# A decode kernel whose cache loads span two heads of one batch, regrouped to one head of both batches

## The chip, the cores and the metric

The kernel runs on one core of one Trainium2 chip. The metric is the time of one execution on the device in microseconds (us); lower is better. The core has five engines: TensorE (PE in the profile), VectorE (DVE), ScalarE (ACT), GpSimd (POOL) and SyncE (SP), and 16 DMA engines that move data between the chip's memory (DRAM tensors) and the on-chip buffers. SP and ACT each issue transfers into a queue of their own.

## The reference

One decoding step of an attention layer followed by a feed-forward layer, for a batch of two, one new token each. All data is float32.

```python
B, Sq, D = 2, 1, 512
H, Sk, Dh = 32, 8192, 128
# k_cache, v_cache: (B, H, Sk, Dh); wq: (D, H*Dh); wo: (H*Dh, D)
q = (layernorm(x) @ wq).reshape(B, Sq, H, Dh).transpose(0, 2, 1, 3)
scores = einsum("bhqd,bhkd->bhqk", q, k_cache) * Dh ** -0.5
o = einsum("bhqk,bhkd->bhqd", softmax(scores), v_cache)
h = x + o.transpose(0, 2, 1, 3).reshape(B, Sq, H * Dh) @ wo
h2 = h + (silu(layernorm(h) @ w_gate) * (layernorm(h) @ w_up)) @ w_down
```

One head of one batch has 8192 x 128 x 4 B = 4 MiB of keys and as much of values. There are 64 such pairs of head and batch, so keys and values together are 512 MiB, and each byte of them is used once. In the cache the batch is the slowest dimension: the heads of one batch lie one behind the other, 4 MiB apart, and the same head of the two batches is 128 MiB apart.

## The kernel before

**Units.** The work on the cache is cut into U = 32 units. A unit is two (head, batch) pairs: 128 partitions, of which the lower 64 hold one pair and the upper 64 the other. Within a pair, the 8192 positions are dealt to 64 partitions, 128 consecutive positions each; so one partition gets one unbroken run of 128 x 128 x 4 B = 64 KiB. Before the change, unit i is the heads 2m and 2m + 1 of batch b, with m = i // 2 and b = i % 2. Since two neighbouring heads of a batch lie one behind the other in the cache, the unit's 128 runs are one unbroken block of 8 MiB.

**Buffers.** Keys have two slots of 8 MiB (`kslot0`, `kslot1`, used in turn), values one (`vslot`). The last unit's values go into a key slot.

**What one unit does.** VectorE multiplies the key tile by the query (L435, two halves), sums over the head's dimension (L439), tells SP that the slot is free (L441, semaphore `kfree`), and takes the maximum (L442, L420). TensorE moves the maxima across partitions (L371 to L374), ScalarE computes the exponentials (L468), TensorE multiplies them with the value tile (`pe_values`, L381), ScalarE tells SP that the value slot is free (L480, semaphore `vfree`), and the result is scaled and written as a column of `oT` (L485). The loops over units are hardware loops; an iteration of VectorE's and ScalarE's holds two units, one for each key slot.

**Before and after the units.** A layer norm and the query projection (L352) fill `qsb`, which holds each query row repeated over the 64 partitions of its pair. After the last unit come the output projection with `wo`, a second layer norm, and the feed-forward layer with `w_gate`, `w_up` and `w_down`; their weights are loaded into the slots as these come free.

**What sets the order.** All large loads stand in one list, and SP issues them one after the other into its one queue (L650): `wq`, the first keys in two halves, then keys of unit i and values of unit i - 1 in turn, the last values, `wo`, `w_gate`, `w_up`, `w_down`. Ahead of a load that overwrites a slot, SP waits for the slot's semaphore (`kfree` or `vfree`); everything behind it in the list waits too. The access pattern of the source is made by `k_src` (L154), for keys and values alike. Of the other transfers, the input `xs` is loaded by ACT (L252) as 2 rows of 2 KiB, and the output is stored by SP and ACT (L657) as 2 rows of 1 KiB each.

Of the kernel before, what the change touches and what calls it, by code (L numbers as in the profile page):

```python
# [4 lines left out]
AF = mybir.ActivationFunctionType  # L5
# [6 lines left out]
P = 128  # L12
# [3 lines left out]
class Program:  # L16
# [22 lines left out]
    def do(self, engine, fn, sem=None, by=1):  # L39

        if sem is None:
            self.steps[engine].append(fn)
            return None
        self.count[sem] += by
        self.steps[engine].append(lambda e: fn(e).then_inc(sem, by))
        return sem, self.count[sem]
# [8 lines left out]
def decode_block(nc, x, k_cache, v_cache, wq, wo, w_gate, w_up, w_down, out):  # L55
    B, _, D = x.shape
    _, H, S, DH = k_cache.shape
    F = w_gate.shape[1]
    assert DH == P and B == 2 and D == 512 and F == 14 * P and H == 32 and S == 64 * P
    DC = D // P  # L60
# [3 lines left out]

    HP = P // 2
    NJ = S // HP
    U = B * H // 2
    LANE = 1
    COLS = (0, 2, 1, 3)
    MQ = H // 2  # L70
    HALF = (slice(0, HP), slice(HP, P))


# [7 lines left out]
    def sbuf(name, *shape, align=32):  # L81
        return nc.alloc_sbuf_tensor(name, list(shape), F32, align_bytes=align).ap()
# [7 lines left out]
    vslot = sbuf("vslot", P, SLOT, align=512)  # L90
# [12 lines left out]
    oT = sbuf("oT", P, H, B)  # L103
    hT = sbuf("hT", P, DC, 32)
    xT = sbuf("xT", P, DC, B)
    osb = sbuf("osb", P, W * DH)
    qsb = sbuf("qsb", P, B, MQ, DH)
    oq = sbuf("oq", P, H, B)
    scores = [sbuf(f"s{n}", P, NJ) for n in range(2)]
    m1 = sbuf("m", P, 1)  # L110
# [24 lines left out]
    wait, do = g.wait, g.do  # L135


    s_dve, s_act, s_pe, s_pool = (g.sem(n) for n in ("dve", "act", "pe", "pool"))
# [13 lines left out]
    loads = []  # L152

    def k_src(cache, i):  # L154
        m, b = divmod(i, B)
        return cache[b, 2 * m : 2 * m + 2].rearrange("h (p j) d -> (h p) (j d)", p=HP)

    v_last = kslot[U % 2]

    def load_kv(kind, i, parts=1):  # L160
        cache, t = (k_cache, kslot[i % 2]) if kind == "k" else (v_cache, vslot if i < U - 1 else v_last)
        n = SLOT // parts
        for c in range(parts):
            own = parts > 1 or (kind, i) == ("v", U - 1)
            sem = alone(f"{kind}{i}_{c}") if own else s_k[i % 2] if kind == "k" else s_v
            loads.append(((kind, i), c, t[:, c * n : (c + 1) * n], k_src(cache, i)[:, c * n : (c + 1) * n], sem))

    loads.append((("wq", 0), 0, vslot, wq.rearrange("(p c) m -> p (c m)", p=P), s_v))
    load_kv("k", 0, 2)
# [132 lines left out]
    _, p = layernorm(xs, [(x_in, 16)])  # L302
# [28 lines left out]
    p = do("vector", lambda e: e.tensor_copy(xT, yt), s_dve)  # L331
# [5 lines left out]
        s_dve,  # L337
    )
    wait("tensor", xb_done, landed[("wq", 0), 0])
    wqv = vslot.rearrange("p (c m k d) -> p c k m d", c=DC, k=2, d=DH)  # L340
    q_done = []
    for n, (m, b) in enumerate((m, b) for m in range(0, MQ, 4) for b in range(B)):
        ps = wide[n % 2].rearrange("p (j d) -> p j d", d=DH)
        if n == 7:
            stop(1)
        if n > 1:
            wait("tensor", q_done[n - 2])
        for c in range(DC):
            for k in range(2):
                p = do(  # L350
                    "tensor",
                    lambda e, ps=ps, c=c, k=k, m=m, b=b: e.matmul(  # L352
                        ps[HALF[k]],
                        xb[:, c * B + b, :],
                        wqv[:, c, k, m : m + 4, :],
                        start=(c == 0),
                        stop=(c == DC - 1),
                    ),
                    s_pe if c == DC - 1 and k == 1 else None,
                )  # L360
        wait("scalar", p)
        q_done.append(
            do("scalar", lambda e, ps=ps, m=m, b=b: e.activation(qsb[:, b, m : m + 4, :], ps, AF.Copy), s_act)
        )
    freed["wq", 0] = p
    wait("tensor", consts_done)

# [58 lines left out]
    def dve_unit(e, b, q, first, done, seen):  # L426
        n = NJ // 2
        s = scores[b]
        for c in range(2):
            if first:  # L430
                e.wait_ge(*landed[("k", 0), c])
            elif c == 0:
                e.wait_ge(s_k[b], 16)
            kt = kslot[b][:, c * n * DH : (c + 1) * n * DH].rearrange("p (j d) -> p j d", d=DH)
            e.tensor_tensor(kt, kt, q.to_broadcast([P, n, DH]), op=OP.mult).then_inc(s_own_dve, 1)  # L435
            if not first:
                (recip if c else biggest)(e, seen + c + 1)
            e.wait_ge(s_own_dve, done + 2 * c + 1)
            e.tensor_reduce(s[:, c * n : (c + 1) * n], kt, axis=AX.X, op=OP.add).then_inc(s_own_dve, 1)  # L439
        e.wait_ge(s_own_dve, done + 4)  # L440
        e.sem_inc(s_kfree, 1)  # L441
        e.tensor_reduce(m1, s, axis=AX.X, op=OP.max).then_inc(s_dve_pe, 1)  # L442

    def dve_rounds(e):
        dve_unit(e, 0, qsb[:, 0, 0:1, :], True, 0, 0)
        e.wait_ge(*q_done[-1])
        e.sem_inc(s_own_dve, -4)
        with nc.Fori(0, U // 2 - 1, engines=[DVE]) as m:  # L448
            dve_unit(e, 1, qsb[:, 1, bass.ds(m, 1), :], False, 0, 0)
            dve_unit(e, 0, qsb[:, 0, bass.ds(m + 1, 1), :], False, 4, 2)  # L450
            e.sem_inc(s_own_dve, -8)
            e.sem_inc(s_pe_dve, -4)
            for k in range(2):
                e.sem_inc(s_k[k], -16)
        dve_unit(e, 1, qsb[:, 1, U // 2 - 1 : U // 2, :], False, 0, 0)
        biggest(e, 3)
        recip(e, 4)

# [19 lines left out]
    def outputs(e, o, told, seen):  # L478
        e.wait_ge(s_pe_act, seen)
        e.sem_inc(s_vfree, 1)  # L480
        e.activation(osb, opart, AF.Copy)  # L481
        e.wait_ge(s_dve_act, told)
        e.activation(rdiag, diag, AF.Copy, scale=r).then_inc(s_act_pe, 1)  # L483
        e.wait_ge(s_pe_act, seen + 1)
        return e.activation(o, ot_ps, AF.Copy)  # L485

    def act_rounds(e):
        with nc.Fori(0, U // 2 - 1, engines=[ACT]) as m:
            for b in range(B):
                softmax(e, b, b + 1, 3 * b + 1)  # L490
                outputs(e, oT[:, bass.ds(m * 2, 2), b], b + 1, 3 * b + 2)
            e.sem_inc(s_own_act, -2)
            e.sem_inc(s_dve_act, -2)
            e.sem_inc(s_pe_act, -6)
        for b in range(B):
            softmax(e, b, b + 1, 3 * b + 1)
            if b:
                e.activation(warm, mhalf[:1, :], AF.Sigmoid)
            last = outputs(e, oT[:, H - 2 :, b], b + 1, 3 * b + 2)
        last.then_inc(s_oT, 1)  # L500

    wait("scalar", consts_done)
# [1 line left out]
    for i in range(U):  # L504
# [5 lines left out]
    p = do(  # L510
        "vector",
        lambda e: e.tensor_tensor(
            om,
            oT.rearrange("p h b -> p b h")[:, :, :, None].to_broadcast([P, B, H, NQ]),
            quarter[:, None, None, :].to_broadcast([P, B, H, NQ]),
            op=OP.mult,
        ),
        s_dve,
    )
    wait("tensor", p)  # L520
    for b in range(B):
        p = do(
            "tensor",
            lambda e, b=b: e.matmul(
                oq_ps[:, b, :], om[:, b].rearrange("p h q -> p (h q)"), fold, start=True, stop=True
            ),
            s_pe if b == B - 1 else None,
        )
    wait("scalar", p)
    p = do("scalar", lambda e: e.activation(oq.rearrange("p c b -> p b c"), oq_ps, AF.Copy), s_act)  # L530
    wait("tensor", p, zeroed)
    for c in range(H):
        for e_, (c0, n) in enumerate(WO):
            if c0 == c:
                wait("tensor", landed[("wo", 0), e_])
        t = c % 4
        p = do(
            "tensor",
            lambda e, c=c, t=t: e.matmul(
                wide[0][32 * t : 32 * t + B, :],  # L540
                oq[:, c, :],
                wo_t[:, c * D : (c + 1) * D],
                start=(c < 4),
                stop=(c >= H - 4),
            ),
# [4 lines left out]
    p = do("scalar", lambda e: e.activation(osb, wide[0], AF.Copy), s_act)  # L550
# [34 lines left out]
    p = project_f(0, gate)  # L585
# [3 lines left out]
    for t in range(4):  # L589
        do(  # L590
            "tensor",
            lambda e, t=t: e.matmul(
                f_ps[32 * t : 32 * t + 32, :], place, h1[:, COLS[t] * P : (COLS[t] + 1) * P], start=True, stop=False
            ),
# [3 lines left out]
    p = do("scalar", lambda e: e.activation(sg, gate, AF.Sigmoid), s_act)  # L598
    wait("vector", p)
    sg_done = do("vector", lambda e: e.tensor_mul(sg, gate, sg), s_dve)  # L600
    p = project_f(DC, up)
# [4 lines left out]
    p = do(  # L606
        "vector",
        lambda e: e.tensor_mul(
            gu.rearrange("p (c j) -> p j c", c=FB),
            up.rearrange("p (j c) -> p j c", c=FB),  # L610
            sg.rearrange("p (j c) -> p j c", c=FB),
        ),
        s_dve,
    )
    gT = rest[:, D + 2 * FQ : D + 3 * FQ]
    wait("vector", p)
    p = do("vector", lambda e: e.transpose(gT, gu), s_dve)
# [3 lines left out]
    for c in range(FB):  # L621
# [3 lines left out]
        for t in range(4):  # L625
            p = do(
                "tensor",
                lambda e, c=c, t=t: e.matmul(  # L628
                    f_ps[32 * t : 32 * t + 32, :],
                    gT[:, c * 32 : (c + 1) * 32],  # L630
                    wd_t[:, c * D + COLS[t] * P : c * D + (COLS[t] + 1) * P],
                    start=False,
                    stop=(c == FB - 1),
                ),
# [73 lines left out]
```

## Time and profile before

| what | value |
|---|---|
| time, median of 3 runs | 1309.12 us (1309.05 to 1309.28) |
| the profiled execution's own time | 1309.09 us |
| its span, first to last instruction | 1307.7 us |
| DMA queue of SP, share of the 16 engines' span | 99.7% |
| bytes moved, mean rate | 564.77 MB, 432 GB/s |
| VectorE busy | 1131.1 us (86%) |
| TensorE busy | 434.1 us (33%) |
| ScalarE busy | 81.0 us (6%) |

The span leaves out 1.39 us of the execution's own time (1309.09 - 1307.7). A row of a group of instructions gives its line, engine, operation, output and inputs, the shape and the count, then the busy time in us and the mean of one in ns, then the idle time of the engine ahead of it and what ended it. "q1" is SP's queue of transfers, "q10" ACT's; packets are what the 16 DMA engines executed, with the small ones counted by size. In the table of stretches the last two columns are the share of the 16 DMA engines that was busy (an average over engines and over the stretch) and the rate in GB/s. In the list of transfers the last column is the median time from issue to landing.

### The profile page before, as it was taken

The numbers are of one execution on the slowest core, as the hardware profiler recorded it, in microseconds if no ns is written. First come the engines' busy times: TensorE is split into PE (matmuls) and PEld (weight loads), VectorE is DVE, ScalarE is ACT, GpSimd is POOL, SyncE is SP. The second block draws the span as 40 slices with busy tenths as digits, with TensorE's granted clock in tenths as the row PEclk, the third lists the DMA queues.
The fourth block names the chain that finished last, engine by engine and source line by source line (L and its number), as shares of the span: only waits on it lengthen the run. The fifth ranks groups of instructions, "written<-read, shape, count | busy, mean of one in ns | idle before, by whom it ended". The sixth has DMA issues, their size and how long they took to land.

```text
span 1307.7 us, 7046 instructions
## 1 busy us (share of the span) xinstructions
PE 434.1 (33%) x2956; PEld 136.0 (10%) x2956; DVE 1131.1 (86%) x246; ACT 81.0 (6%) x272; POOL 3.1 (0%) x15
## 2 busy tenths in 40 slices
PE   2633223333213333322333321333331233332177
PEld 1210001011001011000101100101100010110022
DVE  0999988899888889888889988888988888998841
ACT  0100000000000000000000000000000000000010
POOL 0000000000000000000000000000000000000000
PEclk9866566666556666556666655666665666665578
DMA  9999999999999999999999999999999999999998
GB/s 402 437 439 431 439 433 435 439 429 439 427 439 427 441 425 441 431 439 431 437 437 431 439 427 439 427 441 425 441 429 441 431 437 437 429 441 427 439 419 377
DMA packets 10963, 564.77 MB, mean 432 GB/s; under 512 B 1222, under 2 KB 1226, under 8 KB 1612
## 3 DMA queue, kind: packets, MB, share of 16 engines
q1 hardware_dynamic: 10948, 564.67, 99.7%
q8 instruction: 5, 0.08, 0.0%
q14 instruction: 2, 0.02, 0.0%
q10 hardware_dynamic: 8, 0.01, 0.0%
HBM read 564.66 MB, written 0.00 MB: 432 GB/s over the span
## 4 chain that ended last, share of the span: by engine, by line
DMA 53%; DVE 45%; PE 1%; issue 0%; DVEq 0%; SPq 0%; ACTq 0%
DMA kslot<-in_A_k_cache_dram 48%; DVE kslot L435 22%; DVE s L439 22%; DMA kslot<-in_A_v_cache_dram 3%; DMA kslot<-in_B_w_down_dram 3%; PE opart L381 1%; DVE gm L420 0%; SPq L650 0%; DVE r L424 0%; PE bank L628 0%; DVEq L435 0%; DVEq L441 0%; DVE kslot L642 0%; DVE m L442 0%; DVEq L448 0%
## 5 line engine op out<-in xcount | busy, mean ns | idle before, releaser
L435 DVE TENSOR_TENSOR kslot<-kslot,qsb 128x8192 f32<-128x8192 f32 x64 | 555.6, 8681 | 108.8 <-DMA kslot<-in_A_k_cache_dram 95.5
L439 DVE TENSOR_REDUCE s<-kslot 128x64 f32<-128x8192 f32 x64 | 555.2, 8675 | 0.1
L381 PE MATMUL opart<-vslot,pz 128*8 128x512 f32 x1984 | 284.6, 738 | 239.9 <-DMA vslot<-in_A_v_cache_dram 239.9
L373 PE MATMUL bank<-gm,nscale 1*64 1x1 f32 x64 | 11.8, 251 | 353.6 <-DVE gm L420 353.6
L381 PEld LDWEIGHTS opart<-vslot,pz 128*8 128x8 f32 x1984 | 55.1, 103 | 443.2 <-DMA vslot<-in_A_v_cache_dram 242.5
L371 PE MATMUL bank<-ident,m 128*1 128x128 f32 x64 | 18.7, 396 | 165.6 <-DVE m L442 165.6
L481 ACT ACTIVATE osb<-opart 128x512 f32<-128x512 f32 x32 | 19.1, 598 | 557.3 <-PE opart L381 557.3
L373 PEld LDWEIGHTS bank<-gm,nscale 1*64 1x64 f32 x64 | 9.1, 200 | 369.6 <-DVE gm L420 369.6
L393 PE MATMUL bank<-rdiag,osb 128*128 128x2 f32 x256 | 34.0, 255 | 40.0 <-ACT rdiag L483 40.0
L465 ACT ACTIVATE nb<-bank 128x1 f32<-128x1 f32 x32 | 5.5, 172 | 541.3 <-PE bank L374 541.3
L393 PEld LDWEIGHTS bank<-rdiag,osb 128*128 128x128 f32 x256 | 31.2, 192 | 69.6 <-ACT rdiag L483 69.6
L376 PE MATMUL bank<-rs,sides 128*128 128x1 f32 x64 | 18.7, 362 | 41.6 <-ACT pz L468 41.6
L352 PE MATMUL wide<-vslot,osb 128*64 128x512 f32 x128 | 29.7, 626 | 3.5 <-DMA vslot<-in_A_wq_dram 3.5
L468 ACT ACTIVATE pz<-s,nb 64x128 f32<-64x128 f32 x64 | 25.6, 400 | 1.4
L376 PEld LDWEIGHTS bank<-rs,sides 128*128 128x128 f32 x64 | 16.0, 310 | 44.3 <-ACT pz L468 44.3
L371 PEld LDWEIGHTS bank<-ident,m 128*1 128x1 f32 x64 | 2.7, 81 | 169.1 <-DVE m L442 169.1
L331 DVE COPY xT<-bank 128x8 f32<-128x8 f32 x1 | 0.2, 167 | 15.7 <-PE bank L297 15.7
L442 DVE TENSOR_REDUCE m<-s 128x1 f32<-128x128 f32 x32 | 9.2, 286 | 4.7
L352 PEld LDWEIGHTS wide<-vslot,osb 128*64 128x64 f32 x128 | 10.3, 145 | 22.0 <-issue 22.0
L468 ACT ACTIVATION_READ_ACCUMULATOR pz<-s,nb 64x1 f32 x64 | 11.9, 186 | 0.0
L374 PE MATMUL bank<-gm,nscale 1*64 1x1 f32 x64 | 11.8, 251 | 0.0
L279 DVE BATCH_NORM_STATS2 ln_stats<-attn 2x6 f32<-2x512 f32 x1 | 0.7, 685 | 12.7 <-PE attn L552 12.7
(65 smaller groups left out, 107.8 us busy)
## 6 DMA issues: line engine op xcount, KB each, us to landing
kslot<-in_A_k_cache_dram SPq DMA_DIRECT2D x2, 4096.0 KB, 37.2
vslot<-in_A_wo_dram SPq DMA_DIRECT2D x1, 5120.0 KB, 21.5
kslot<-in_B_w_gate_dram SPq DMA_DIRECT2D x1, 3584.0 KB, 31.5
kslot<-in_B_w_up_dram SPq DMA_DIRECT2D x2, 1792.0 KB, 37.3
vslot<-in_A_wo_dram SPq DMA_DIRECT2D x1, 3072.0 KB, 28.4
kslot<-in_B_w_down_dram SPq DMA_DIRECT2D x2, 1024.0 KB, 31.1
kslot<-in_B_w_down_dram SPq DMA_DIRECT2D x1, 768.0 KB, 33.5
kslot<-in_B_w_down_dram SPq DMA_DIRECT2D x1, 512.0 KB, 34.3
```

Source lines behind the costliest of these rows:

```text
L352: lambda e, ps=ps, c=c, k=k, m=m, b=b: e.matmul(ps[HALF[k]], xb[:, c * B + b, :], wqv[:, c, k, m : m + 4, :], start=(c == 0), stop=(c == D ...
L371: e.matmul(mrow, m1, ident, start=True, stop=True).then_inc(s_pe_dve, 1)
L373: e.matmul(nb_ps[HALF[0]], nscale, gm[:, 0:1], start=True, stop=True)
L374: e.matmul(nb_ps[HALF[1]], nscale, gm[:, 1:2], start=True, stop=True).then_inc(s_pe_act, 1)
L376: e.matmul(den, sides.rearrange("p w a -> p (w a)"), rs, start=True, stop=True).then_inc(s_pe_dve, 1)
L381: inst = e.matmul(opart[32 * t : 32 * t + 2 * W, :], pz[:, w, :], t_v[:, w * W * DH : (w + 1) * W * DH], start=(w < 4), stop=(w >= NW - 4),)
L393: inst = e.matmul(ot_ps, osb[:, a * DH : (a + 1) * DH], rdiag[:, a::W], start=(a == 0), stop=(a == W - 1))
L435: e.tensor_tensor(kt, kt, q.to_broadcast([P, n, DH]), op=OP.mult).then_inc(s_own_dve, 1)
L439: e.tensor_reduce(s[:, c * n : (c + 1) * n], kt, axis=AX.X, op=OP.add).then_inc(s_own_dve, 1)
L442: e.tensor_reduce(m1, s, axis=AX.X, op=OP.max).then_inc(s_dve_pe, 1)
L468: inst = e.activation(pz[h, :, k * W : (k + 1) * W], s[h].rearrange("p (w a) -> p w a", a=W), AF.Exp, bias=nb[h], scale=SCALE, accum_out=r ...
L481: e.activation(osb, opart, AF.Copy)
```

## The change

A unit becomes one head of both batches: unit i is head i, the lower 64 partitions hold batch 0 and the upper 64 hold batch 1. The queries are laid out to match (`qsb` by head, the batch chosen by the half of the partitions), and a unit's two output columns are now the two batches of one head, which lie side by side in `oT`. The number of units, the number of transfers, their sizes, the 64 KiB runs, the slots, the semaphores and the order of every engine's instructions stay as they are.

The source of a cache load is no longer one block: it is an access pattern with three dimensions, 2 batches (128 MiB apart), 64 runs each (64 KiB apart), 16384 elements.

```diff
-    U = B * H // 2
+    U = H
-    MQ = H // 2
...
-    qsb = sbuf("qsb", P, B, MQ, DH)
+    qsb = sbuf("qsb", P, H, DH)
...
     def k_src(cache, i):
-        m, b = divmod(i, B)
-        return cache[b, 2 * m : 2 * m + 2].rearrange("h (p j) d -> (h p) (j d)", p=HP)
+        return cache[:, i].rearrange("b (p j) d -> b p (j d)", p=HP)
...
-            loads.append(((kind, i), c, t[:, c * n : (c + 1) * n], k_src(cache, i)[:, c * n : (c + 1) * n], sem))
+            dst = t[:, c * n : (c + 1) * n]
+            loads.append(((kind, i), c, dst, k_src(cache, i)[:, :, c * n : (c + 1) * n], sem))
...
-    wqv = vslot.rearrange("p (c m k d) -> p c k m d", c=DC, k=2, d=DH)
+    wqv = vslot.rearrange("p (c h d) -> p c h d", c=DC, d=DH)
...
-    for n, (m, b) in enumerate((m, b) for m in range(0, MQ, 4) for b in range(B)):
+    for n, h in enumerate(range(0, H, 4)):
...
-            for k in range(2):
+            for b in range(B):
...
-                        ps[HALF[k]],
+                        ps[HALF[b]],
                         xb[:, c * B + b, :],
-                        wqv[:, c, k, m : m + 4, :],
+                        wqv[:, c, h : h + 4, :],
...
-            dve_unit(e, 1, qsb[:, 1, bass.ds(m, 1), :], False, 0, 0)
-            dve_unit(e, 0, qsb[:, 0, bass.ds(m + 1, 1), :], False, 4, 2)
+            dve_unit(e, 1, qsb[:, bass.ds(m * 2 + 1, 1), :], False, 0, 0)
+            dve_unit(e, 0, qsb[:, bass.ds(m * 2 + 2, 1), :], False, 4, 2)
...
-                outputs(e, oT[:, bass.ds(m * 2, 2), b], b + 1, 3 * b + 2)
+                outputs(e, oT[:, bass.ds(m * 2 + b, 1), :].rearrange("p o b -> p (o b)"), b + 1, 3 * b + 2)
...
-            last = outputs(e, oT[:, H - 2 :, b], b + 1, 3 * b + 2)
+            last = outputs(e, oT[:, H - 2 + b, :], b + 1, 3 * b + 2)
```

On SP's queue, where all large loads are issued, the list began like this before (a row is a transfer: its line, the buffer it writes, the tensor it reads, and the shape on the side that it writes):

```order
L650 DMA vslot<-in_A_wq_dram 128x16384
L650 DMA kslot0<-in_A_k_cache_dram 128x8192 x2
L650 DMA kslot1<-in_A_k_cache_dram 128x16384
L650 DMA vslot<-in_A_v_cache_dram 128x16384
L650 DMA kslot0<-in_A_k_cache_dram 128x16384
```

and begins like this with the change:

```order
L647 DMA vslot<-in_A_wq_dram 128x16384
L647 DMA kslot0<-in_A_k_cache_dram 128x1x8192 x2
L647 DMA kslot1<-in_A_k_cache_dram 128x1x16384
L647 DMA vslot<-in_A_v_cache_dram 128x1x16384
L647 DMA kslot0<-in_A_k_cache_dram 128x1x16384
```

No transfer moved or was added. The written side of the cache loads got a dimension of size 1, so that both sides have three; the read side, which these rows do not show, is 2 x 64 x 16384 where it was 128 x 16384.

At the end of SP's list the last values and the weights stand in both kernels in the same order, and the weights' shapes are unchanged. Before:

```order
L650 DMA vslot<-in_A_v_cache_dram 128x16384
L650 DMA kslot0<-in_A_v_cache_dram 128x16384
L650 DMA vslot<-in_A_wo_dram 128x10240
L650 DMA vslot<-in_A_wo_dram 128x6144
L650 DMA kslot1<-in_B_w_gate_dram 128x7168
L650 DMA kslot1<-in_B_w_up_dram 128x3584 x2
```

and with the change:

```order
L647 DMA vslot<-in_A_v_cache_dram 128x1x16384
L647 DMA kslot0<-in_A_v_cache_dram 128x1x16384
L647 DMA vslot<-in_A_wo_dram 128x10240
L647 DMA vslot<-in_A_wo_dram 128x6144
L647 DMA kslot1<-in_B_w_gate_dram 128x7168
L647 DMA kslot1<-in_B_w_up_dram 128x3584 x2
```

Only the two cache loads differ; the weights still have 128 rows on both sides.

More of the change, by code (lines that the diff above doesn't have):

```diff
@@ L348, in decode_block @@
         for c in range(DC):
-            for k in range(2):
+            for b in range(B):
                 p = do(
                     "tensor",
-                    lambda e, ps=ps, c=c, k=k, m=m, b=b: e.matmul(
-                        ps[HALF[k]],
+                    lambda e, ps=ps, c=c, h=h, b=b: e.matmul(
+                        ps[HALF[b]],
                         xb[:, c * B + b, :],
-                        wqv[:, c, k, m : m + 4, :],
+                        wqv[:, c, h : h + 4, :],
                         start=(c == 0),
@@ L358, in decode_block @@
                     ),
-                    s_pe if c == DC - 1 and k == 1 else None,
+                    s_pe if c == DC - 1 and b == B - 1 else None,
                 )
         wait("scalar", p)
-        q_done.append(
-            do("scalar", lambda e, ps=ps, m=m, b=b: e.activation(qsb[:, b, m : m + 4, :], ps, AF.Copy), s_act)
-        )
+        q_done.append(do("scalar", lambda e, ps=ps, h=h: e.activation(qsb[:, h : h + 4, :], ps, AF.Copy), s_act))
     freed["wq", 0] = p
@@ L444, in dve_rounds @@
     def dve_rounds(e):
-        dve_unit(e, 0, qsb[:, 0, 0:1, :], True, 0, 0)
+        dve_unit(e, 0, qsb[:, 0:1, :], True, 0, 0)
         e.wait_ge(*q_done[-1])
@@ L454, in dve_rounds @@
                 e.sem_inc(s_k[k], -16)
-        dve_unit(e, 1, qsb[:, 1, U // 2 - 1 : U // 2, :], False, 0, 0)
+        dve_unit(e, 1, qsb[:, U - 1 :, :], False, 0, 0)
         biggest(e, 3)
```

## The prediction, as put on record before the run

> **What bounds the kernel now.** I read the page first (slices, DMA queues), then the chain of work in order of time, then what SP's queue waits for.
>
> ```profile
> span 1307.7 us, 7046 instructions
> ...
> PE 434.1 (33%) x2956; PEld 136.0 (10%) x2956; DVE 1131.1 (86%) x246; ACT 81.0 (6%) x272; POOL 3.1 (0%) x15
> ...
> DMA  9999999999999999999999999999999999999998
> GB/s 402 437 439 431 439 433 435 439 429 439 427 439 427 441 425 441 431 439 431 437 437 431 439 427 439 427 441 425 441 429 441 431 437 437 429 441 427 439 419 377
> DMA packets 10963, 564.77 MB, mean 432 GB/s; under 512 B 1222, under 2 KB 1226, under 8 KB 1612
> ...
> q1 hardware_dynamic: 10948, 564.67, 99.7%
> q8 instruction: 5, 0.08, 0.0%
> q14 instruction: 2, 0.02, 0.0%
> q10 hardware_dynamic: 8, 0.01, 0.0%
> ```
>
> The reader is to see that VectorE, the busiest engine, is idle for 14% of the span, while the 16 DMA engines have no idle slice: SP's queue alone keeps them busy for 99.7% of the span. The chain, in the middle of the run, looks at first as if VectorE shared the bound:
>
> ```profile
> 368.13 42.26 DMA kslot<-in_A_k_cache_dram
> ...
> 410.53 8.69 DVE kslot L435
> ...
> 419.41 8.59 DVE s L439
> 428.00 8.60 DVE kslot L435
> ...
> 436.68 8.65 DVE s L439
> ...
> 445.41 42.26 DMA kslot<-in_A_k_cache_dram
> ```
>
> From 368.13 to 445.41 lie 77.28 us and two units, so four loads of 8 MiB: 19.32 us each, which is 434 GB/s. That is the full rate of the slices above. VectorE's work between the two key loads runs beside value loads; the chain only passes through it. So the span is the time that the DMA engines need for their bytes, and anything that changes their rate moves the end one for one.
>
> One engine's rate follows from the q1 row and the span: 564.67 MB / (16 x 0.997 x 1307.7 us) = **27.07 GB/s for a busy engine**. A 64 KiB run takes it 65,536 B / 27.07 GB/s = 2.421 us. A cache load of 128 runs is 8 runs on each of 16 engines: 8 x 2.421 = 19.37 us, against the 19.32 us seen in the chain.
>
> **The change part by part.** Instructions, their order, waits, sizes and run lengths stay. What changes on the path is the shape of the source of 65 transfers (31 whole key loads and 2 halves, 32 value loads): the outermost dimension was 128 on both sides, and is now 2 on the side that is read. So the question is how a transfer is dealt out to the 16 engines, and the packet counts of before answer part of it.
>
> ```profile
> kslot<-in_A_k_cache_dram SPq DMA_DIRECT2D x31, 42.3
> vslot<-in_A_v_cache_dram SPq DMA_DIRECT2D x31, 29.3
> ...
> xs<-in_A_x_dram ACTq DMA_DIRECT2D x1, 4.0 KB
> ...
> out_dram<-kslot SPq DMA_DIRECT2D x1, 2.0 KB
> out_dram<-kslot ACTq DMA_DIRECT2D x1, 2.0 KB
> ```
>
> The program has 76 transfers with 128 rows (33 of keys, 32 of values, 1 + 2 of `wq` and `wo`, 8 of the feed-forward weights) and three with 2 rows (`xs` and the two stores above). Suppose each leaves one packet for each row, and a small one for each engine that took part, to report the end. With 16 reports from a transfer of 128 rows and 2 from one of 2 rows, that makes 76 x 16 + 3 x 2 = 1,222 small packets and 76 x 128 + 3 x 2 = 9,734 rows; with the 5 + 2 packets of instructions, 10,963. The page has 1,222 under 512 B and 10,963 in all: exact on both. ACT's queue alone agrees: `xs` and one store are 4 rows and 4 reports, the 8 packets of q10. So a transfer whose outermost dimension is 2 was dealt to 2 engines, although each of its `xs` rows, 2 KiB long, could have been cut. The deal goes by whole slices of the outermost dimension.
>
> With the change the outermost dimension is 2 where the transfer reads and 128 where it writes. No transfer of before has unequal ones, so two ends bound this: the 128 decides and 16 engines work as now, or the 2 decides and two engines move one batch each. I take the second. The read side has only two slices to give away, and the nearest rows, the three transfers with a 2, went to two engines. [...]
>
> **The sum.** Each of the two engines now gets 64 runs of a cache load where it got 8: 56 x 2.421 = 135.6 us more, for 64 loads' worth of bytes (two half loads make one). 64 x 135.6 = 8,677 us. The loads all stand in one queue on the same two engines, so nothing overlaps it. Span: 1307.7 + 8,677 = 9,985 us. With the 1.39 us around the span (1309.09 for that execution, which is 0.03 us under the median), **9,986 us**, 7.6 times the time before.
>
> What could add to it or hide in it:
>
> *The rate of a busy engine while 14 others stand idle* is not seen over a long stretch. It can be bounded. The tail has stretches in which the engines run out one by one:
>
> ```profile
> 1302.00:1303.00 1.00, 1.00 (x44) 1.00 (x40) 0.00 (x0) 0.00 (x0) 0.00 (x0) 1.00 0.99 406
> ...
> 1304.00:1305.00 1.00, 0.58 (x22) 0.31 (x17) 0.00 (x0) 0.00 (x0) 0.00 (x0) 1.00 0.22 86
> ```
>
> At a share of 0.99 the rate is 406 / (16 x 0.99) = 25.6 GB/s for a busy engine; at a share of 0.22 (3.5 engines on average) 86 / (16 x 0.22) = 24.4. An engine is not faster for having fewer neighbours, so the 27.07 looks like its own limit and not a sixteenth of a shared one. These are the short rows of the last weights, so the 64 KiB value stays 27.07. Each of the two engines has 64 loads x 4 MiB = 268.4 MB; the rest of the span is 1307.7 - 64 x 19.37 = 68 us. The fastest slice above, 441 GB/s over 16 engines, gives 27.6 GB/s: 268.4 / 27.6 = 9,726 us, with 68 + 1.4 about 9,795. At 25.6 it is 10,485 + 69 = 10,555. At 24.4, rows of 2 KiB, it would be 11,070; I leave that out as too short a row to stand for these. [...]
>
> *Gaps in the queue.* Ahead of a value load SP waits until the values before it are used up (`vfree`).
>
> ```profile
> SPq L650 <- ACTq L480: 982.5, 32, 32.8
> SPq L650 <- DVEq L441: 209.5, 32, 14.6
> ...
> L381 PE MATMUL opart<-vslot,pz 128*8 128x512 f32 x1984 | 284.6, 738 | 239.9 <-DMA vslot<-in_A_v_cache_dram 239.9
> ...
> L435 DVE TENSOR_TENSOR kslot<-kslot,qsb 128x8192 f32<-128x8192 f32 x64 | 555.6, 8681 | 108.8 <-DMA kslot<-in_A_k_cache_dram 95.5
> L439 DVE TENSOR_REDUCE s<-kslot 128x64 f32<-128x8192 f32 x64 | 555.2, 8675 | 0.1
> ```
>
> Behind that wait stand the next key load and all later ones. The wait ends some 9 us after the values land (L381: 284.6 us over 31 units). In that time the key load issued just before is still under way: 64 x 2.421 = 154.9 us of cover for 9 us of work, so the gap costs nothing; without cover it would be 9 x 32 = 290 us. The `kfree` wait needs VectorE's 555.6 + 555.2 us over 32 units, 34.7 us, against 309.8 us for a unit's two loads. The 982.5 us of waiting at L480 should grow to about 32 x 300 us and still cost nothing.
>
> *The tail.* `wo`, gate and up have 128 rows on both sides and keep 16 engines. Their parts on 14 engines land while the last values still come; those on the two busy engines queue behind, 8 rows each as before, so the tail after the last values stays as it is.
>
> *The rest* (queries by head at L352, 128 matrix products as before; the two columns of `oT` side by side; one index for `qsb`) has the same instruction counts, and lies beside the first key load, whose halves now take 77 us each, or beside later loads. Nothing.
>
> **The rivals.**
>
> *All 16 engines still work.* This is the case on the other side: the deal goes by the written side's 128, or the two read dimensions count as 2 x 64. It decides if any of that happens ahead of the deal. Then a load stays at 19.37 us, VectorE and the queue see nothing new, and the time stays at 1309 us. The lower and upper partitions then read 128 MiB apart instead of 4 MiB, in the same 64 KiB runs; I give that nothing, with a few us either way. For it: no row shows unequal dimensions. Against it: the 2-row transfers above. 0.05.
>
> *Two engines, but each faster.* If 432 GB/s were a shared ceiling and an engine alone could do twice its sixteenth, 268.4 / 54.1 = 4,961 us, with the rest 5,031. Against it is the 24.4 GB/s at a share of 0.22. 0.03 for anything below my range that is still slower than before.
>
> *Two engines, and each slower, or one engine.* The two batches are read in step, 128 MiB apart; should they meet in the same part of the memory and halve each other, 268.4 / 13.5 + 69 is about 19,950 us, and the same if one engine got all 128 runs. Against it: the two halves of a load were a power of two apart before (4 MiB), at the full rate. 0.05 for anything above the range.
>
> **How the numbers follow.** The forecast has 0.87, and the range 9,750 to 10,560 us takes the rates of 27.6 and 25.6 GB/s with a little room below. Slower by over 0.2% (2.6 us, about what a measurement of this kernel can tell from no change) is all of it but the first rival: 0.87 + 0.03 + 0.05, and 0.01 of that rival's 0.05 for a slightly worse pattern: 0.96. Of what is left, 0.03 is no change and 0.01 faster.
>
> **What would show it.** In the profile after: SP's queue at about an eighth of 16 engines (a mean share near 0.13: the same engine time as now, 16 x 0.997 x 1307.7 = 20,860 us, over 16 x 9,985 = 159,760 us), 57 GB/s over the span, a cache load about every 155 us; the packets under 512 B down by 65 x 14 to 312, while the rows stay 9,734; VectorE at 1,131 us still, now 11% of the span; key loads and value loads nearly the whole chain. Sixteen reports for each load, or slices above 100 GB/s in the middle, would prove the step about the deal wrong; 312 small packets with a time far from 9,986 would prove the rate wrong.

## The result

| | before | with the change |
|---|---|---|
| time, median | 1309.2 us (1309.05 to 1309.42, 4 runs) | 9995.88 us (9994.72 to 9996.11, 4 runs) |
| span of the profiled execution | 1307.7 us | 9994.6 us |
| mean rate of the transfers | 432 GB/s | 57 GB/s |

The change makes the kernel slower by a factor of 7.635, 95% interval 7.622 to 7.648. Forecast were 9,986 us, with a range of 9,750 to 10,560.

The page of the changed kernel, its head and its transfers:

```profile
span 9994.6 us, 7046 instructions
...
PE 425.7 (4%) x2956; PEld 135.5 (1%) x2956; DVE 1131.3 (11%) x246; ACT 80.8 (1%) x272; POOL 3.1 (0%) x15
...
DMA  1111111111111111111111111111111111111113
GB/s 84 54 55 54 55 54 55 54 55 54 55 54 55 54 55 54 55 54 55 54 55 54 55 54 55 54 55 54 55 54 54 54 54 54 54 54 54 54 54 114
DMA packets 10053, 564.77 MB, mean 57 GB/s; under 512 B 312, under 2 KB 316, under 8 KB 702
...
q1 hardware_dynamic: 10038, 564.66, 13.3%
...
another core or an unknown queue 88%; DVE 11%; DMA 0%; issue 0%; PE 0%; DVEq 0%; ACT 0%; POOL 0%; SPq 0%; ACTq 0%; POOLq 0%
...
L432 DVE TENSOR_TENSOR kslot<-kslot,qsb 128x8192 f32<-128x8192 f32 x64 | 555.6, 8681 | 8489.7 <-DMA kslot<-in_A_k_cache_dram 8489.7
```

The bytes are the same and so is the engines' own work (VectorE 1131.3 us, before 1131.1). What fell is the share of the 16 DMA engines, from 99.7% to 13.3%: 16 x 0.133 = 2.1 engines on average. The small packets fell from 1,222 to 312, and that is 14 fewer for each of the 65 cache loads. The first and the last slice, in which the weights are loaded, are the only ones above 55 GB/s. The chain can't name the load that VectorE waits for ("an unknown queue", 88%); the row of L432 does: it waits 8,489.7 us for keys. In order of time the middle of that chain reads:

```profile
5003.20 273.21 another core or an unknown queue
...
5276.57 8.69 DVE kslot L432
...
5311.79 273.66 another core or an unknown queue
...
5621.24 273.21 another core or an unknown queue
```

From 5003.20 to 5621.24 are 618.04 us for two units, four loads: 154.5 us each, where before it was 19.32.

### The profile page after: what moved, and what is told of

Read it like the earlier page. It is cut to its first block, busy times and chain, and to the rows that moved or that the text cites. A ratio compares the mean times of both kernels' runs of the same rounds, so it can differ in the third digit from the quotient of the medians.

```text
span 9994.6 us, 7046 instructions
## 1 busy us (share of the span) xinstructions
PE 425.7 (4%) x2956; PEld 135.5 (1%) x2956; DVE 1131.3 (11%) x246; ACT 80.8 (1%) x272; POOL 3.1 (0%) x15
## 3 DMA queue, kind: packets, MB, share of 16 engines
q1 hardware_dynamic: 10038, 564.66, 13.3%
## 4 chain that ended last, share of the span: by engine, by line
another core or an unknown queue 88%; DVE 11%; DMA 0%; issue 0%; PE 0%; DVEq 0%; ACT 0%; POOL 0%; SPq 0%; ACTq 0%; POOLq 0%
DVE kslot L432 5%; DVE s L436 5%; DMA kslot<-in_B_w_down_dram 0%; PE opart L378 0%; DVE gm L417 0%; DVE m L439 0%; DVEq L432 0%; DVE r L421 0%; DVEq L445 0%; ACT pz L465 0%; SPq L647 0%; PE bank L373 0%; PE bank L625 0%; PE bank L390 0%
## 5 line engine op out<-in xcount | busy, mean ns | idle before, releaser
L432 DVE TENSOR_TENSOR kslot<-kslot,qsb 128x8192 f32<-128x8192 f32 x64 | 555.6, 8681 | 8489.7 <-DMA kslot<-in_A_k_cache_dram 8489.7
```

## Experiments

In all of them the kernel before was run beside, at 1308.7 to 1309.2 us. Each experiment is one run, except where two are named.

**Is it the shape of the read side, or the two batches?** The kernel before with its own units, but with the 128 runs of a load taken from 2 slices of the same batch:

```diff
-        return cache[b, 2 * m : 2 * m + 2].rearrange("h (p j) d -> (h p) (j d)", p=HP)
+        rows = cache[b].rearrange("h (p j) d -> (h p) (j d)", p=HP)
+        return rows.rearrange("(o u p) x -> u o p x", o=2, p=P // 2)[m]
```

> The kernel before, its units and queries grouped as before, but each cache load reads 2 slices of 64 runs that lie 64 MiB apart in the same batch (so a unit gets other heads' rows than its queries belong to; the amount of work is the same). If the shape of the read side decides (2 slices, 2 engines), it takes 9,986 to 9,996 us, with 312 packets under 512 B. If the regrouping by batches or the distance of 128 MiB between them slowed the change, this stays near 1309 us with 1,222 small packets.

Measured: 9,994.68 us, with this line on its page:

```profile
DMA packets 10053, 564.77 MB, mean 57 GB/s; under 512 B 312, under 2 KB 316, under 8 KB 702
```

No batch is mixed here, and the slices lie half as far apart. The packets are the change's, and the time is within 1.2 us of it. So the loss comes with an outermost dimension of 2 on the read side; whether the 2 slices are two batches or two parts of one batch makes no difference.

**How does it go with the number of slices?** The same edit with `o=16` and `o=32`, then with 4 and 8.

> As the run with 2 slices, but 16 slices of 8 runs, 8 MiB apart (again other rows than the queries', the same amount of work). By the number of slices alone all 16 engines work: 1,222 small packets and 1309 us. A second theory, from the last value load of the changed kernel, which took 190 us instead of 154.5 while 14 other engines wrote weights: engines that write certain partitions at the same time halve each other. Here an engine has 8 neighbouring partitions, and if each engine has one such partner, the time is 68 + 64 x 8 x 4.842 = 2,547 us, still with 1,222 small packets.

> As the run with 16 slices, but 32 slices of 4 runs, 4 MiB apart. By the number of slices alone (32 is dealt to 16 engines): 1309 us, 1,222 small packets. It is the control for the run with 16 slices: if that is slow because the reads are scattered, this one is as slow or slower (2,547 us); if it is slow because of which partitions an engine writes, this one can be at 1309 us, provided that two slices of 4 partitions fall to an engine in the way that they do for 128 rows.

> The kernel before with loads that read 4 slices of 32 runs, 32 MiB apart (other rows than the queries', the same amount of work). 312 + 65 x 2 = 442 small packets by the number of slices. By the number of engines alone: 32 runs each, 68 + 64 x 32 x 2.421 = 5,026 us. If partitions 32 apart share a path, engines 0 and 1, and 2 and 3, meet in every run, at the 5.04 us a run seen with 16 slices: 68 + 64 x 32 x 5.04 = 10,390 us, slower than with two engines.

> The same with 8 slices of 16 runs, 16 MiB apart. 312 + 65 x 6 = 702 small packets by the number of slices. By the number of engines alone: 16 runs each, 68 + 64 x 16 x 2.421 = 2,547 us. If partitions 32 apart share a path, engines e and e + 2 meet: 68 + 64 x 16 x 5.04 = 5,229 us.

| slices | engines by the small packets | time, us | by the number of engines alone | if partners always meet |
|---|---|---|---|---|
| 2 | 2 (312) | 9,994.68 | 9,986 | 9,986 |
| 4 | 4 (443) | 5,271.16 | 5,026 | 10,390 |
| 8 | 8 (702) | 4,647.98 | 2,547 | 5,229 |
| 16 | 16 (1,222) | 2,652.63 | 1,309 | 2,547 |
| 32 | 16 (1,222) | 1,317.58 | 1,309 | 1,309 |

In the last column the run of 64 KiB is priced at 4.842 us for 16 slices (twice 2.421, as on record before that run) and at 5.04 us for 4 and 8, which is what the run with 16 slices then gave: (2,651.1 - 68) / (64 x 8), from its span. That partitions 32 apart make partners was the author's assumption there, and for 2 and 32 slices the column assumes that none meet. The program of loads alone, further down, shows partners in one place, 0 to 31 with 32 to 63 (27 GB/s together), and none in 32 to 63 with 64 to 95 (52 GB/s).

The packets confirm the deal at all five sizes (443 is one more than computed; SP's own queue fits exactly, with 10,168). But the time doesn't follow the number of engines. With 16 slices all 16 engines are busy, and move half of what they should:

```profile
DMA  9999999999999999999999999999999999999999
GB/s 274 210 209 208 208 207 206 213 208 209 209 207 206 210 210 210 207 209 206 209 210 210 207 209 207 206 212 209 209 208 208 206 211 209 210 207 208 207 209 337
DMA packets 10963, 564.77 MB, mean 213 GB/s; under 512 B 1222, under 2 KB 1226, under 8 KB 1612
...
q1 hardware_dynamic: 10948, 564.67, 100.0%
```

The first slice (`wq`) and the last (the other weights), where transfers still have 128 rows, are faster with the same engines. Scattered reads are not the cause: 32 slices, scattered twice as finely, run at

```profile
DMA packets 10963, 564.77 MB, mean 429 GB/s; under 512 B 1222, under 2 KB 1226, under 8 KB 1612
```

(Its 1,317.58 us are still 0.7% above the kernel before; the reason is open.) So a second theory was needed, and the one on record before the runs was that engines which write certain partitions at the same time halve each other. With 16 slices an engine has 8 neighbouring partitions. The run with 4 slices shows how such meeting goes. Its rate over the span, in 40 slices of 132 us:

```profile
GB/s 121 68 71 80 93 106 109 107 109 108 109 109 107 109 107 109 108 109 109 107 109 107 109 107 109 109 107 109 107 109 107 109 109 108 109 107 109 107 128 147
```

The transfers are alike from start to end, yet the four engines begin at 68 GB/s, 17 each, climb for some 800 us, and then stay at 109, 27.2 each. This refutes the price that I had put on it (every run at 5.04 us, 10,390 us). The reading that fits is that partners meet only while they are in step, and that these two pairs drifted out of it; no view shows single engines, so the drift itself is not shown. With 8 slices the rate rises and falls again, by the same reading as the pairs drift out of step and back:

```profile
GB/s 165 107 109 108 108 109 109 115 115 116 118 112 116 117 116 118 122 130 134 134 129 141 152 156 146 150 107 116 117 119 125 115 104 108 107 105 106 104 113 162
```

**Can the regrouping be had at 16 engines?** The plain repair is to issue each load as two transfers, one for each batch, with 64 rows on both sides:

```diff
-            loads.append(((kind, i), c, dst, k_src(cache, i)[:, :, c * n : (c + 1) * n], sem))
+            for k, h in enumerate(HALF):
+                loads.append(((kind, i), c, dst[h], k_src(cache, i)[k, :, c * n : (c + 1) * n], sem))
```

(the waits for `s_k` and `s_v` count 32 instead of 16).

> The change with each cache load issued as two transfers of 64 partitions, one for each batch, so that both sides have 64 as outermost dimension. By the number of slices: 16 engines with 4 runs each, twice, so 19.37 us for both, 1309 us; the packets under 512 B rise to 130 x 16 + 11 x 16 + 6 = 2,262. If it is the reading of two batches that is slow, 9,996 us as in the change. If engines that write the same 64 partitions at once halve each other, it lies between 1309 and 2,547 us, by how far the engines get out of step.

Measured: 2,656.17 us, 4% above the upper end of what was expected, at

```profile
DMA packets 12004, 564.78 MB, mean 213 GB/s; under 512 B 2262, under 2 KB 2266, under 8 KB 2652
...
q1 hardware_dynamic: 11988, 564.67, 100.0%
```

The 2,262 reports say that 16 engines take part; they are busy for 100.0% of the span, and again at half the rate. This repair gives back most of the loss, and is still twice the time of before.

**Is it the meeting?** If it is, the same transfers must run faster when the engines are put out of step. For this the halves were cut so that, by the deal of whole slices, engine e writes the partitions 4e to 4e + 3 of a half (another order of a head's positions; the result stays):

```diff
-        return cache[:, i].rearrange("b (p j) d -> b p (j d)", p=HP)
+        return cache[:, i].rearrange("b (r o j) d -> b o r (j d)", r=4, o=16)
```

> The change with each load as two transfers of 64 partitions, as the run before it with halves, but each now reads 16 slices of 4 runs (the positions of a head are dealt to the partitions in another order, which leaves the result as it is), so that engine e writes the 4 partitions 4e to 4e + 3 of the half. It is the control for the run with a head start. By the number of slices alone: 16 engines, 1309 us. [...]

Measured: 2,653.01 us, not the 1309 us by the number of slices; the other order of the halves took 2,656.17. To that kernel a head start was added, by cutting `wq` alone into six transfers (their count on `s_v` becomes 96):

```diff
-    loads.append((("wq", 0), 0, vslot, wq.rearrange("(p c) m -> p (c m)", p=P), s_v))
+    wq_rows = wq.rearrange("(p c) m -> p (c m)", p=P)
+    for part in [slice(r, 32, 4) for r in range(4)] + [HALF[1], slice(32, 64)]:
+        loads.append((("wq", 0), 0, vslot[part], wq_rows[part], s_v))
```

> The same transfers of keys and values as the control, byte for byte and in the same order. Only the first load of the program, wq, is issued in another cut: first four transfers of 8 rows each, which go to 8 engines, then the other 96 rows to all 16. This leaves half of the engines 4 runs, 9.7 us, behind the others from the start. If partner engines meet because they write the same half in step, they now write different halves for the whole run: 1309 to 1400 us. If the halves are slow for another reason (two transfers for a load, 64 partitions at a time, reads from two batches), the 9.7 us change nothing: about 2,650 us.

Measured: 2,249.98 us. Nothing in the 512 MiB of keys and values was changed, and the time falls by 15%. So the loss depends on when the engines write and not only on what, as the meeting would have it; that a load is two transfers of 64 partitions doesn't explain it, since it still is. But the size was missed by far (1309 to 1400 us was forecast). SP's waits on this run offered a reason:

```profile
SPq L650 <- PE wide L354: 76.2, 1, 76.2
```

Ahead of the first values SP waits for the query projection, behind two key loads only, and an engine that is ahead can run out of work there. The next run gives the head start later, with the first value load (for this, the loads of unit 0 keep the order of positions of the first run with halves, and TensorE waits once for the four added transfers):

```diff
+                if (kind, i, k) == ("v", 0, 0):
+                    for r in range(4):
+                        loads.append(((kind, i), "first", dst[r:32:4], src[r:32:4], s_first))
+                    loads.append(((kind, i), c, dst[32:HP], src[32:], sem))
```

> The run with a head start gained less than expected (2,250 us), and its trace offers a reason: SP waited 76 us for the query projection before it could issue the first values, the queue ran empty, and all engines set out together again. Here the head start is given after that point: of the first value load the lower half goes out as four transfers of 8 rows (8 engines) and one of 32 rows (all 16), so that 8 engines are 4 runs behind from there on; wq is one load again. If meeting in step is the cause, rows take 2.42 us from then on and the time is 1309 to 1400 us. If the first head start was not lost but a difference of 4 runs is simply worth no more, it is 2,250 us again; without any effect 2,650 us.

Measured: 1,904.3 us, at a mean of 297 GB/s against 251 and 213:

```profile
GB/s 293 214 198 298 287 287 309 287 287 306 289 292 303 292 291 299 292 303 295 288 302 306 310 326 321 299 331 288 317 299 311 306 309 296 315 293 309 309 270 348
```

Better again, and still far from the 1309 to 1400 us that were forecast. A third run doubles the head start, by cutting both halves of that load.

> As the second run with a head start, but both halves of the first value load are cut that way, so 8 engines are sent 8 runs more than the others. For partners that are x us of work apart (0 to 9.68), a half load of 4 runs takes 19.36 - x. With the first head start half loads took 17.0 us (x = 2.4) and with the second 14.1 us (x = 5.3, where 9.7 was meant). If the same part, 0.55, of the 19.4 us now given is kept, x = 10.6, of which 9.68 is a full half load and 0.9 us meets again: half loads of about 10.6 us, 64 x 21.2 + 68 = 1,425 us. If all of it is kept, the partners are in step again: 2,650 us. If the gain has another reason than the distance, about 1,900 us.

Measured: 1,964.87 us; the forecast of 1,425 was wrong, by more than the run before it. The stretches from 160 us show a part of the reason (the two last columns are the DMA engines' share and GB/s):

```profile
160.00:171.00 11.00, 1.55 (x8) 0.88 (x8) 8.11 (x2) 1.15 (x5) 0.00 (x0) 0.50 0.75 125
171.00:185.00 14.00, 10.14 (x67) 2.22 (x68) 14.00 (x4) 0.90 (x2) 0.00 (x0) 0.70 0.47 201
185.00:200.00 15.00, 1.28 (x9) 0.70 (x8) 9.38 (x3) 0.17 (x1) 0.00 (x0) 0.54 1.04 301
```

and beside them the chain of the same stretch:

```profile
173.73 9.84 PE opart L388 x64
183.59 0.02 ACTq L488
183.63 0.54 SPq L658
```

From 171 us on about half of the engines stand still (0.47), until SP issues the second values at 183.63, which it may do only when the first are used up. The engines that were ahead have to wait there for the others, so much of the head start is lost again. How much can't be read from these rows well enough: 14 us of standing still would leave 5.4 of the 19.4 us, close to the 5.3 that the run before it kept by its time, and this would account for times so near to each other (1,904 and 1,965). But the row before, at 0.75, has idle time too, and with it 0.25 x 11 + 0.53 x 14 = 10.2 us of all 16 engines are idle, an estimate of 20 us for half of them, which would leave nothing.

The rival on record for this run, that the gain has another reason than the distance between partners (about 1,900 us), came nearer than the forecast, and it stays open. A head start that lasts wasn't tried, so it is not shown either that 16 engines out of step reach 1309 us in this form. What is shown is that the time falls from 2,653 to 1,904 us though the loads of units 1 to 31 keep their sizes, places and order: it depends on how a few transfers ahead of them are dealt. A distance between partner engines is the reading that fits, and what it would bring was forecast wrong three times.

**Do they meet where they read or where they write?** In the runs with slices, which parts an engine reads and which partitions it writes changed together. One more program loads the same sources twice, into two places:

```diff
+    for first in (0, P // 4):
+        for i in range(8):
+            if p is not None:
+                g.wait("sync", p)
+            p = g.do("sync", lambda e, i=i, first=first: e.dma_start(t[first : first + HP], src(i)), s_load, 16)
```

> A program of loads alone, everything else of the kernel left out (its output is just the input x). Sixteen loads of 2 slices of 32 runs (4 MiB, two engines), one after the other: eight into partitions 0 to 63, so that the two engines write 0 to 31 and 32 to 63, then the same eight sources again into partitions 32 to 95, so that they write 32 to 63 and 64 to 95. Only the written side differs. If partners meet where they write, and partitions 32 apart share a path while 64 to 95 is another, the first eight take up to 32 x 5.04 = 161 us each (less as far as the engines fall out of step) and the last eight 32 x 2.42 = 77.4 us. If the engines meet where they read, both eights take the same time.

Measured: 1,880.2 us. Two stretches of its span, the DMA engines' share and GB/s last, and what SP waited for (in total, times, longest):

```profile
600.00:1200.00 600.00, 0.00 (x0) 1.00 0.12 27
...
1260.00:1800.00 540.00, 0.00 (x0) 1.00 0.12 52
...
SPq L73 <- DMA t<-in_A_k_cache_dram: 1786.2, 15, 157.8
SPq L75 <- DMA t<-in_A_k_cache_dram: 79.6, 1, 79.6
```

Into partitions 0 to 31 and 32 to 63 the two engines together move 27 GB/s, one engine's worth, and a load takes up to 157.8 us. Into 32 to 63 and 64 to 95 they move 52 GB/s, and the last load takes 79.6 us. The sources and the share of the engines (0.12, two of 16) are the same. So these two engines meet where they write. (The slow eight came first; the other order was not run.)

**Where did the last value load lose 35 us?** The change's end has a stretch that the prediction had not:

```profile
9613.88 143.29 another core or an unknown queue
9757.22 9.87 PE opart L378 x64
...
9772.16 175.06 another core or an unknown queue
9947.26 8.73 PE opart L378 x64
```

The values before the last landed at 9757.2, the last at 9947.2: 190.0 us for a load that takes 154.5. In that time `wo`, gate and up were on their way on the other engines. The run that holds them back (the part of the line that differs):

```diff
-("wo", 0): ("v", U - 2), ("wf", 0): ("k", U - 1)
+("wo", 0): ("v", U - 1), ("wf", 0): ("v", U - 1)
```

> The change, with the loads of wo, gate and up held back until the last values are used up. In the changed kernel the last value load took 190 us instead of 154.5, in the stretch in which 14 engines brought these weights. If those writes slowed the two engines, the last load takes 154.5 us again, all weights then load at 16 engines in 45 us behind it, and the time falls to 9,975 to 9,981 us. If the last value load is slow for another reason (it is the only one that goes to a key slot), it still takes 190 us, and the weights come on top: about 10,010 us.

Measured: 9,972.33 us (two runs, 9,971.8 and 9,972.86). The chain has

```profile
9757.14 9.61 PE opart L378 x64
...
9771.81 139.78 another core or an unknown queue
9911.63 9.16 PE opart L378 x64
9920.86 0.34 SPq L647
...
9924.78 42.83 DMA kslot<-in_B_w_down_dram
```

so the last load is back at 9911.6 - 9757.1 = 154.5 us, and all weights follow, from the first issue at 9920.9 to the last landing at 9967.6 in 47 us (425 GB/s from 9925 to 9965). The weights' transfers had slowed the two engines; that they did so by meeting them where they write is the reading from the other runs.

## Why the prediction was right, point by point

*The deal.* Right: the 2 on the read side decides. 312 small packets were forecast and found, 9,734 rows stayed, and the share of 16 engines is 0.133 against 0.13. The trace of before had no unequal dimensions and could not show it; the packets of the five runs with 2 to 32 slices do (312, 443, 702, and twice 1,222).

*The rate of a lone engine.* Right to 0.3%: 154.5 us for a load against 154.9, so 27.1 GB/s with 14 engines idle. That the 27.07 is an engine's own rate and not a sixteenth of a shared one, taken from the tail's rows, held.

*The sum.* The span came out at 9,994.6 against 9,985. Two terms were off, and they nearly cancel: 64 loads at 154.51 us instead of 154.94 are 28 us less, and the last value load at 190.0 instead of 154.5 is 35.5 us more. That the total is off by less than either of them is luck.

*The tail.* The step that failed: it said that the weights' parts on 14 engines land beside the last values at no cost. They landed beside them, and made the last load 35.5 us longer. The run with the weights held back puts 23.6 us of 9,995.9 to it (35.5 us won on the last load, the rest lost again by loading the weights behind it). What follows the last values was as before, 9994.6 - 9947.2 = 47.4 us against 1307.7 - 1260.4 = 47.3.

*Gaps in the queue.* Right: the slices of the middle never fall below 54 GB/s. The waiting at the `vfree` wait, though, was forecast at 32 x 300 us:

```profile
SPq L647 <- ACTq L477: 5492.2, 32, 181.9
...
5131.87 0.50 SPq L647 DMA_DIRECT2D vslot<-in_A_v_cache_dram  x1
5132.42 131.47 SPq L647 DMA_DIRECT2D kslot<-in_A_k_cache_dram  x1
```

Most of the rest of a unit's 309 us SP spends in issuing: a key load behind an unfinished value load held it for 131.47 us, where an issue took 0.33 us before:

```profile
406.80 0.33 SPq L650 DMA_DIRECT2D kslot<-in_A_k_cache_dram  x1
```

It cost nothing here, since the queue was full.

*The rivals.* All 16 engines at work did not happen, and neither did a doubling or a halving of the engines' rate. The halving was laid to the memory that is read. A halving exists, but where partitions are written (27 GB/s against 52 in the program of loads alone), and it doesn't strike the change's two engines against each other: one writes 0 to 63, the other 64 to 127, and each ran at 27.1 GB/s.

## What to carry to other kernels

Before a load's source gets a new outermost dimension, look at its size: in these runs a transfer was dealt to engines by whole slices of the outermost dimension, and a 2 there left two engines (312 small packets, 9,994.68 us), though the other side had 128 (the runs had the small number on the side that reads). The small packets on the page, counted against the number of transfers, show the deal without a trace of the engines. And a DMA share of 100% isn't yet full rate: read the GB/s beside it, because engines can be busy for twice as long over the same bytes, as 16 slices against 32 show (208 against 429 GB/s), and as two engines do that write partitions 0 to 31 and 32 to 63 at the same time (27 GB/s together, against 52 in other places).

## What the runs showed that was not expected

**Two engines that wrote partitions 0 to 31 and 32 to 63 at the same time had one engine's rate together.** They moved 27 GB/s, and 52 GB/s into 32 to 63 and 64 to 95. On 16 engines, transfers of 64 partitions ran at 208 GB/s (two orders, 2,656 and 2,653 us), those of 128 partitions in 16 slices too (2,653 us), and in 32 slices at 429. At 208 GB/s each engine was busy (a share of 100.0%), at half the rate. That this loss is the one of the two places is a reading, and the range of partitions alone doesn't explain it: 16 slices write all 128 and ran at 208 too, and with the second head start transfers of 64 partitions moved 287 to 331 GB/s in the slices of the middle. Which partitions meet was measured at the two places only.

**The loss depends on the moment, not on the shape alone.** Four engines went from 68 to 109 GB/s within a run; 16 slices never left 206 to 213; and a few transfers dealt otherwise, once near the start, changed the whole run by up to 28% (2,653 to 1,904 us). Why some patterns speed up within a run and others never do is open.

**An issue can hold SP for long.** The 131.47 us above end when about 5 runs of the key load in transfer are left (it lands at 5276.4, 12.5 us later, at 2.42 us each), with 64 + 64 behind them: an estimate of some 133 runs outstanding at one engine. But gate and up were held up too, while the 16 engines were busy for 0.68 of the time (9770 to 9870), and then no engine had more than 64 runs of values and 8 rows of each of the five weight loads, 104 in all. So a fixed number of runs doesn't explain both, and what ends an issue is open:

```profile
9768.81 36.45 SPq L647 DMA_DIRECT2D kslot<-in_B_w_gate_dram  x1
9805.31 52.38 SPq L647 DMA_DIRECT2D kslot<-in_B_w_up_dram  x2
```
